# A two-layer memory-recurrent transformer block on Trainium2: the set-up's small transposes and first loads are moved, the weight loads are regrouped, and a new order table is used

## The chip, the core and the metric

The kernel runs on one NeuronCore of a Trainium2 chip. The metric is device time in microseconds (us) of one execution, from the runs' own timer; a profile of one further execution shows each engine's instructions. Engines: PE (matrix multiplications), DVE and ACT (vector and scalar work, here mostly copies out of PSUM, the layer norms and the softmaxes), POOL, and SP, which here only issues DMAs. DMAs move data between HBM and SBUF, or inside SBUF; some of them transpose on the way.

## The reference, cut to what matters

```python
def A(x, mem0):                      # 64 segments of 32 rows, one after the other
    mem = mem0                       # 8 rows
    for s in range(64):
        h = concat(mem, x[32*s:32*s+32])          # 40 x 448
        q, k, v = h @ Wq, h @ Wk, h @ Wv          # 16 heads of 256
        o = softmax(mask(q @ k.T / 16)) @ v @ Wo
        mem = o[:8];  out[32*s:32*s+32] = o[8:]
def B(x):                            # gated MLP, 448 -> 1792 -> 448
    return (relu(x @ W_gate) * (x @ W_up)) @ W_down
x = x + A(ln(x));  x = x + B(ln(x));  x = x + A(ln(x));  x = x + B(ln(x))    # x: 2048 x 448
```

The memory that segment s hands to segment s+1 makes A a recurrence: the second pass of A can only follow the first one, four segments behind.

## The kernel before

**Folded weights.** Each head's scores are h Wq Wk^T h^T, and each head's output is P h Wv Wo. So a *set-up* multiplies the weights once: 128 matmuls make M = Wq Wk^T (`prodM`), 128 make N = Wv Wo (`prodN`), each in four *quarters* of four heads. `products` (called in `setup`, L801 to L869) makes two products of a pair of heads at a time; a quarter is 24 matmuls on the whole PE array and 8 on half of its columns, and needs a quarter of both weights. The products are copied out of PSUM by ACT and DVE (L730, L731).

**Loads of the set-up.** Wq, Wk and Wv are loaded by transposing DMAs into eight slots of the tile `big` (`wT`, issued on L806), Wo by plain ones (`wo`, L810). A quarter is 0.9 MB. All are issued by SP, whose queue is in order: an instruction that waits holds back those behind it. Between the first loads SP also issues the first 64 rows of x (L788), the memory's two pieces (L789, L790), the transpose of the memory (L791), of the first normalised rows (L925, in `ln_a`) and of the first h (L1059, in `h_nat`). PE's work on a quarter of M waits for that quarter of Wq and of Wk.

**Steps.** After the set-up 68 steps follow; step t does segment t of the first layer and segment t-4 of the second. A step makes TT = M h (`t_units`: matmuls `P<-hT,Mw` and `P<-hT,M`), the scores of the memory rows (`P<-hT,TTm`) and of the segment rows (`P<-hT,TTs`), softmaxes on DVE and ACT, the memory's output (`P<-ident,Pm`, `P<-PTm,hK`, `P<-Nw,UTm`: "ptm", "umem" and "unm" below), its transpose back into hT (`P<-selm,X`, "mt"), and the segment's output (`P<-PTs,hK`, and for two steps at once `P<-Nw,big`). Each pair of steps also takes a tile of 128 rows through the MLP (`P<-xBT,big`, `P<-big,hB`). The next step's t_units need mt's result. In steps 12 to 59 the pattern repeats every four steps.

**What sets the order.** Each operation is recorded (`_Order.add`) with an estimated duration; a planner (`_Order.run`) then lays them out engine by engine. On PE the order goes by a table `RANK` written into the file, one number for each kind of operation and place; DVE, ACT, POOL and SP take, of the operations ready within `SLACK` ns, the one with the highest priority, which `BIAS` shifts by kind. An operation that may run on ACT or DVE goes to the one that the planner has free first. The engines then run their lists in order and wait for each other by semaphores. All PE instructions are written on L135.

**Tile forms.** PE's array is used whole (128*128 in the profile), as two halves of 64 rows (64*128), as two halves of columns (128*64) or as four strips of 32 columns (128*32); matmuls on different parts run at the same time. The planner's `mode` tells these apart.

**Transposes.** Rows and columns are exchanged either by a DMA that transposes, or on PE by a matmul with an identity matrix (`transposed`, L1048), whose result DVE copies out of PSUM. Before, PE does this only for tiles of the last steps.

Of the kernel before, what the change touches and what calls it, by code (L numbers as in the profile page):

```python
# [7 lines left out]
BF = dt.bfloat16  # L8
# [164 lines left out]
class _Order:  # L173
# [238 lines left out]
BIAS = {'dnE': 3176.0, 'glE': -82836.0, 'hk': 20613.0, 'init': 13859.0, 'lna': 7507.0, 'lnaC': -13533.0, 'lnaT': -43908.0, 'lnb': 29243.0, 'lnbT':  # L412
    -1363.0, 'load': 14359.0, 'mem': -10045.0, 'mt': -1168.0, 'mtE': 18941.0, 'prodE': -35100.0, 'ptmE': 12133.0, 'pts': -3736.0, 'ptsE': -5023.0,
    'ride': -1141.0, 'rt': -20763.0, 'rtT': -24105.0, 'smx': 110515.0, 'ssx': -8015.0, 'tEm': -15380.0, 'tEs': -51468.0, 'umE': -46772.0, 'usE':
    -102462.0, 'wg': -1137.0, 'x': -3626.0, 'xE': 55107.0, 'xb': -35016.0, 'yE': -13006.0, 'ys': 8416.0}
SLACK = {"pe": 108.0, "act": 154.0, "dve": 264.0, "pool": 233.0, "sp": 156.0}
PERIOD = 88192
RANK = {'dn.1': (-104610, 108209, -90484, -82188, -75463, -89082, -42692), 'dn.3': (-145101, -63706, -147288, -87906, -65974, -148521, -105677),
    'dn.e-1': (-141783, -142922, -108237, -138993, -143563, -144358, -145977), 'dn.e-3': (-104113, -71161, -102721, -97163, -97947, -76248, -66681),
    'dn.e1': (-82612, -70713, -79787, -45174, -88781, -40934, -62418), 'dnc.e1': (-96652, -57589, -80514, -147771, -97522, -72425, -17242), 'dnc.e3':  # L420
    (-146846, -103333, -121313, -81992, -86751, -107795, -123988), 'dnc.r1': (-117628, -111364, -73352, -38397, -118907, -118093, -32712), 'dnc.r3':
    (-143017, -137155, 18497, -94398, -143254, -115919, -116884), 'dnc.r5': (-106807, -76746, -107659, -97861, -105664, -60991, -110757), 'dnc.r7':
    (-144792, -138828, -146554, -77829, -119011, -118053, -123462), 'glF0.1': (-96461, -101197), 'glF0.3': (-127779, -127536), 'glF0.e-1': (-124566,
    -135911), 'glF0.e-3': (-95498, -95971), 'glF0.e1': (-31142, -52941, -93058, -94243), 'glF0.e3': (-100249, -61034), 'glF0.r1': (-112765, -113170),
    'glF0.r3': (-132135, -137757), 'glF0.r5': (-103453, -104429), 'glF0.r7': (-129942, -128688), 'glF1.1': (-21437, -96883), 'glF1.3': (-129957,
    -130626), 'glF1.e-1': (-128167, -130286), 'glF1.e-3': (-42210, -99667), 'glF1.e1': (-74197, -74754, -92380, -92606), 'glF1.e3': (-117239,
    -111385), 'glF1.r1': (-114358, -112556), 'glF1.r3': (-64652, -135836), 'glF1.r5': (-103077, -104009), 'glF1.r7': (-126468, -72866), 'glF2.1':
    (-99406, -102205), 'glF2.3': (-30063, -137144), 'glF2.e-1': (-135080, -136315), 'glF2.e-3': (-86341, -50884), 'glF2.e1': (-69414, -83802, -95776,
    -90525), 'glF2.e3': (-123487, -131166), 'glF2.r1': (-106583, -115805), 'glF2.r3': (-46676, -98801), 'glF2.r5': (-81661, -106213), 'glF2.r7':
    (-134619, -88043), 'glF3.1': (1334, -600), 'glF3.3': (-15610, -49583), 'glF3.e-1': (-67322, -113701), 'glF3.e-3': (-72200, -95812), 'glF3.e1':  # L430
    (-76155, -75823, -92586, -94517), 'glF3.e3': (-107149, -141187), 'glF3.r1': (-58559, -114450), 'glF3.r3': (-137836, -137979), 'glF3.r5': (-73882,
    -77471), 'glF3.r7': (-130187, -128436), 'glH0.1': (-95004,), 'glH0.3': (-126217,), 'glH0.e-1': (-125385,), 'glH0.e-3': (-95255,), 'glH0.e1':
    (-76562, -92759), 'glH0.e3': (-101751,), 'glH0.r1': (-111534,), 'glH0.r3': (-134652,), 'glH0.r5': (-102256,), 'glH0.r7': (-126926,), 'glH1.1':
    (-98081,), 'glH1.3': (-125139,), 'glH1.e-1': (-125229,), 'glH1.e-3': (-99371,), 'glH1.e1': (-73456, -90480), 'glH1.e3': (-21565,), 'glH1.r1':
    (-111459,), 'glH1.r3': (-137215,), 'glH1.r5': (-102039,), 'glH1.r7': (-131203,), 'glH2.1': (-95573,), 'glH2.3': (-136318,), 'glH2.e-1':
    (-133204,), 'glH2.e-3': (-102542,), 'glH2.e1': (-79422, -92762), 'glH2.e3': (-21556,), 'glH2.r1': (-115069,), 'glH2.r3': (-139483,), 'glH2.r5':
    (-102571,), 'glH2.r7': (-133536,), 'glH3.1': (-104497,), 'glH3.3': (-130453,), 'glH3.e-1': (-130004,), 'glH3.e-3': (-103143,), 'glH3.e1': (-73596,
    -43078), 'glH3.e3': (-95245,), 'glH3.r1': (-112910,), 'glH3.r3': (-136600,), 'glH3.r5': (-105539,), 'glH3.r7': (-127975,), 'lnbT.e3': (-97266,),
    'mt.0': (-48556,), 'mt.1': (-73646,), 'mt.2': (-87524,), 'mt.3': (-111081,), 'mt.e-1': (-110824,), 'mt.e-2': (-85897,), 'mt.e-3': (-72736,),
    'mt.e-4': (-46901,), 'mt.e0': (-47132,), 'mt.e1': (-64122,), 'mt.e2': (-82778,), 'mt.r0': (-116855,), 'mt.r1': (-91632,), 'mt.r2': (-103650,),  # L440
    'mt.r3': (-124373,), 'mt.r4': (-56759,), 'mt.r5': (-10709,), 'mt.r6': (-91148,), 'mt.r7': (-111361,), 'prodM.r0': (7632, 8758, 3519, 18670,
    -18035, -8559, -19521, 22221, 506, 0, 29137, -16498, 23379, -13694, -14382, -8950, -10525, -16874, -19468, -19177, 16859, -17615, -19884, -20323,
    -14282, -19681, -10489, -17286, -21816, -21722, -21526, -21195, -23854, -22964, -26122, -20647, -22523, -24653, -20618, -21769, -20688, -25891,
    -30330, -28270, -28128, -29016, -29523, -37170, -26079, -29040, -31310, -35312, -29785, -36941, -29896, -27348), 'prodN.r0': (-44880, -39246,
    -42485, -45500, -43952, -42650, -38039, -4352, -42711, 17370, -35502, -48417, -46709, -57726, -46225, -49325, -39689, -14687, -3938, -48290,
    -57916, -59747, -35946, 21060, -51553, -27452, -46795, -34885, -52124, -55744, -51211, -53783, -42693, -26175, -59523, -53826, -58085, -57316,
    -38263, -59020, -41416, -59756, -60059, -53961, -62863, -56473, -38442, -70119, -68178, -57790, -58316, -67893, -41999, -49426, -68908, -58622),
    'ptm.0': (-41321,), 'ptm.1': (-59656,), 'ptm.2': (-78783,), 'ptm.3': (-98083,), 'ptm.e-1': (-98891,), 'ptm.e-2': (-77845,), 'ptm.e-3': (-60297,),
    'ptm.e-4': (-41694,), 'ptm.e0': (-38279,), 'ptm.e1': (-55288,), 'ptm.e2': (-75058,), 'ptm.r0': (-51324,), 'ptm.r1': (-72642,), 'ptm.r2':
    (-98342,), 'ptm.r3': (-114034,), 'ptm.r4': (-49435,), 'ptm.r5': (-57665,), 'ptm.r6': (-86733,), 'ptm.r7': (-103757,), 'pts.e3': (-95739,),  # L450
# [912 lines left out]
```

## Time and profile before

| | |
|---|---|
| median of 6 runs | 1508.49 us (1504.79 to 1510.80) |
| the profiled execution: its own time | 1512.58 us |
| its span, first to last instruction | 1510.8 us |
| PE busy | 1459.3 us, 97% of the span |
| ACT, DVE busy | 802.8 us (53%), 778.0 us (51%) |
| idle time of PE that a wait for Wk's loads ended | 20.7 us, in 4 waits |
| first "unm" (`P<-Nw,UTm`) starts | 78.59 us |

The profile lists, by line and engine, how long instructions ran and what ended the idle time before them. Its timeline gives the start of each group of like instructions; "SPq" there is an issue by SP's queue, and its duration is that of issuing, not of the transfer. The chain of waits follows the run back from its last instruction. A view of windows gives each engine's busy time and PE's granted clock in a stretch (1.00 is full speed, 0.50 half). A busy PE isn't a PE at its peak, since the ends of matmuls are modelled; the distance between starts is what shows its pace.

### The profile page before, as it was taken

What the parts mean: (1) busy time and instruction counts of PE and PEld (TensorE: products, weight loads), DVE (VectorE), ACT (ScalarE), POOL (GpSimd) and SP (SyncE); (2) the same over time, 40 slices, a digit from 0 to 9 for tenths busy, and PEclk for the clock granted to TensorE, in tenths of its full rate; (3) what the DMA queues carried; (4) which work ended last, traced back from release to release, by engine and by line L of the source; (5) the groups of instructions that cost most, each with busy time, mean ns of one, the idle gap of its engine ahead of it and who ended that gap; (6) DMA issues with size and microseconds to landing.
All of it is one profiled execution on the core that took longest, in us unless ns stands there. A gap on an engine that the chain in (4) does not pass through costs nothing.

```text
span 1510.8 us, 79648 instructions
## 1 busy us (share of the span) xinstructions
PE 1459.3 (97%) x37086; PEld 1163.8 (77%) x37086; DVE 778.0 (51%) x2033; ACT 802.8 (53%) x2436; POOL 38.6 (3%) x86
## 2 busy tenths in 40 slices
PE   5889899999999999999999999999999999999997
PEld 2467778788878778788878778888878878887775
DVE  4434554555455455645455554545555555545553
ACT  4744556456554555556455545546455545645342
POOL 2000000000000000000000000000000000000000
PEclk9989999999999999999999999999999999999998
DMA  9942212112121121111121111111111111122121
GB/s 204 222 131 34 23 34 27 30 21 32 27 33 25 29 31 29 25 21 34 30 30 25 29 31 28 25 25 34 30 28 27 28 30 23 29 25 32 24 31 16
DMA packets 187547, 60.23 MB, mean 40 GB/s; under 512 B 176313, under 2 KB 186321, under 8 KB 187217
## 3 DMA queue, kind: packets, MB, share of 16 engines
q1 hardware_dynamic: 187216, 55.15, 20.8%
q8 instruction: 291, 4.77, 1.3%
q14 instruction: 40, 0.32, 0.1%
HBM read 10.33 MB, written 1.84 MB: 8 GB/s over the span
## 4 chain that ended last, share of the span: by engine, by line
PE 90%; DVE 3%; DMA 3%; SPq 2%; ACT 1%; issue 0%; POOL 0%
PE P L135 90%; SPq L806 2%; DMA PTs<-Ps 1%; DMA stg<-xnA 1%; DMA big<-in_A_Wk_dram 1%; DMA xBT<-xnB 1%; DVE XF L1215 1%; DVE stat L911 0%; ACT Mw L730 0%; DVE X L1129 0%; DVE hT L731 0%; DVE XA L1286 0%; DVE XB L1217 0%; DVE stat L984 0%; DVE big L731 0%
## 5 line engine op out<-in xcount | busy, mean ns | idle before, releaser
L135 PE MATMUL P<-hT,Mw 128*128 128x80 bf16 (+1 forms) x11424 | 423.4, 200 | 2.2 <-issue 2.0
L135 PEld LDWEIGHTS P<-hT,Mw 128*128 128x128 bf16 x11424 | 403.0, 100 | 12.1 <-issue 2.2
L730 ACT ACTIVATE TTs<-P 128x384 bf16<-128x384 f32 (+3 forms) x653 | 294.3, 451 | 0.0
L135 PE MATMUL P<-Nw,big 128*32 128x448 bf16 x5488 | 282.4, 353 | 0.5 <-issue 0.4
L730 ACT ACTIVATE TTm<-P 128x96 bf16<-128x96 f32 (+2 forms) x652 | 158.0, 242 | 171.0 <-PE P L135 160.4
L730 ACT ACTIVATE big<-P 128x512 bf16<-128x512 f32 (+1 forms) x367 | 185.0, 545 | 105.6 <-PE P L135 105.3
L135 PEld LDWEIGHTS P<-Nw,big 128*32 128x32 bf16 x5488 | 139.8, 97 | 98.7 <-issue 3.8
L135 PE MATMUL P<-xBT,big 128*128 128x128 bf16 (+3 forms) x3920 | 213.1, 216 | 1.5 <-DMA xBT<-xnB 0.9
L135 PEld LDWEIGHTS P<-xBT,big 128*128 128x128 bf16 (+1 forms) x3920 | 185.3, 98 | 19.5 <-issue 5.7
L135 PE MATMUL P<-Nw,UTm 128*32 128x224 bf16 x7504 | 194.3, 261 | 1.0 <-ACT UTm L730 0.6
L135 PEld LDWEIGHTS P<-Nw,UTm 128*32 128x32 bf16 x7504 | 179.9, 98 | 14.4 <-issue 4.3
L731 DVE CAST big<-P 128x512 bf16<-128x512 f32 (+1 forms) x145 | 87.7, 615 | 102.9 <-PE P L135 101.4
L1251 ACT ACTIVATE gT<-P 128x512 bf16<-128x512 f32 (+2 forms) x140 | 71.0, 509 | 91.7 <-DVE hB L1252 60.3
L984 DVE TENSOR_REDUCE stat<-P 128x2 f32<-128x80 f32 (+1 forms) x67 | 15.7, 234 | 196.6 <-PE P L135 195.2
L135 PE MATMUL P<-hT,M 64*128 64x80 bf16 (+1 forms) x3808 | 93.8, 197 | 8.7 <-DVE hT L731 4.3
L135 PEld LDWEIGHTS P<-hT,M 64*128 64x128 bf16 x3808 | 75.7, 96 | 27.1 <-issue 7.0
L135 PE MATMUL P<-big,hB 128*128 128x448 bf16 (+1 forms) x574 | 96.4, 354 | 0.0
L1129 DVE TENSOR_TENSOR X<-P,XH 32x224 bf16<-32x224 f32 x134 | 51.1, 381 | 87.3 <-ACT XH L1126 85.1
L135 PE MATMUL P<-PTs,hK 64*128 64x512 bf16 (+1 forms) x640 | 87.1, 338 | 3.5 <-DMA PTs<-Ps 3.3
L1126 ACT ACTIVATE XH<-P 64x224 f32<-64x224 f32 x67 | 23.6, 352 | 120.1 <-PE P L135 120.1
L1252 DVE TENSOR_TENSOR hB<-gT,P 128x512 bf16<-128x512 bf16 (+2 forms) x140 | 76.7, 575 | 17.8 <-ACT gT L1251 14.3
L135 PE MATMUL P<-big 128*128 128x448 bf16 (+1 forms) x256 | 50.7, 384 | 20.7 <-DMA big<-in_A_Wk_dram 20.7
(89 smaller groups left out, 1155.6 us busy)
## 6 DMA issues: line engine op xcount, KB each, us to landing
big<-in_A_Wo_dram SPq DMA_DIRECT2D x4, 896.0 KB, 7.1
XA<-in_A_x_dram SPq DMA_DIRECT2D x32, 56.0 KB, 2.3
out_dram<-ys SPq DMA_DIRECT2D x32, 56.0 KB, 2.3
big<-in_B_W_down_dram SPq DMA_DIRECT2D x2, 784.0 KB, 6.6
big<-in_B_W_gate_dram SPq DMA_DIRECT2D x3, 448.0 KB, 4.4
big<-in_B_W_up_dram SPq DMA_DIRECT2D x3, 448.0 KB, 4.2
hK<-hT SPq DMA_TRANSPOSE x68, 2.8
PTs<-Ps SPq DMA_TRANSPOSE x67, 3.0
```

Source lines behind the costliest of these rows:

```text
L135: ins = E.matmul(out, lhsT=lhsT, rhs=rhs, **kw)
L730: return E.activation(out(), src(), ACT.Copy)
L731: return E.tensor_copy(out(), src())
L806: wload(f"w{k}" + ("ab"[half] if half is not None else ""), lambda E: E.dma_start_transpose(dst, W[:, c:c + w]), [("slot", i, j) for i in ...
L984: S.dve(kind, lambda E: E.tensor_reduce(st[:, so:so + n], src(), AX.X, ALU.max), w, rd, [(pre, 0)])
L1126: S.act("xE", lambda E: E.activation(S.XH[64:128, :], T.b()[64:128, 0:224], ACT.Copy), 224, T.res(BOTQ), [("XH",)])
L1129: S.dve("xE", lambda E, r=r, r2=r2, c=c: E.tensor_tensor(S.X[r, c], T.b()[r, 0:224], S.XH[r2, :], ALU.add), 224, T.res((j,)) + [("XH",)], ...
L1215: S.dve("xb", lambda E: E.tensor_tensor(S.XF[r, :], T.b()[r, 0:D], S.XA[cols, q, :], ALU.add), D, T.res((TOPQ, BOTQ)[h]) + [("XA", q, l)], ...
L1251: S.act("glE", lambda E, G=G, k=k, w=w: E.activation(S.gT[:, k % 2, 0:w * n], G.b()[:, 0:w * n], ACT.Relu), w * n, G.res(), [("gT", k % 2)])
L1252: S.dve("glE", lambda E, V=V, k=k, w=w, a=a: E.tensor_tensor(S.hB[:, a:a + w, 0:n], S.gT[:, k % 2, 0:w * n].rearrange("p (i x) -> p i x", ...
```

## The change

- The first rows of x and the memory's two pieces are issued on ACT's queue instead of SP's, ahead of ACT's other work.
- The memory, the first normalised rows and the first h are transposed on PE (16, 128 and 128 columns at a time, five matmuls each) with a copy by DVE, instead of by DMAs that SP issues. `transposed` learns a form of 16 rows.
- Wq and Wk are loaded quarter by quarter in turn, instead of Wq's last two quarters in one; the last quarter of Wk comes in two halves with a semaphore each. Wv's first two quarters are two loads, with Wo's first two between them. The planner's estimates for loads are changed.
- `BIAS`, `SLACK` and `RANK` are replaced, and so is the order of all engines' instructions throughout the run. What is computed stays.

In the order as built, matmul by matmul: in steps 12 to 59 PE's 2188 matmuls of four steps are the same, in another order. SP's list in the set-up is Wq, Wk, Wq, Wk, Wq, Wk, Wq, Wk's two halves, a quarter of Wv, two of Wo, two of Wv, then PTs<-Ps of step 0 (L1052, waits for DVE), then the last two of Wo and Wv's halves. PE's list begins with the memory's five transposes, then the whole first quarter of M (24 and 8 matmuls), and goes on quarter by quarter; after M it does all of step 0's t_units and both its scores before N begins. Before, PE left the first quarter of M after 8 matmuls for one that needed the second.

```diff
+BIAS = {'dnE': 2862.0, 'first': 1181.0, 'glE': -38535.0, 'hk': 28128.0, 'hkE': 15263.0, 'init': 27046.0, 'lnaC': 24960.0, 'lnaT': 1106.0, 'lnaTE':
...
-SLACK = {"pe": 108.0, "act": 154.0, "dve": 264.0, "pool": 233.0, "sp": 156.0}
+SLACK = {"pe": 108.0, "act": 130.0, "dve": 225.0, "pool": 426.0, "sp": 337.0}
...
-        def small():
-            wload("x0", lambda E: E.dma_start(S.XA[0:64, 0, :], S.x_d[0:64, :]), [("XA", 0, 0)], 300.0, 2300.0)
...
-            S.dma("mem", "mT", lambda E: E.dma_start_transpose(S.mTc[:, :, :], mN), [("gT", 0), ("gT", 1)], [("mTc",)], 500.0, 6500.0, base=1e9)
+        def first(name, fn, wr):
+            S.dma("first", name, fn, (), wr, 500.0, 2600.0, "act", base=1e9)
+        first("x0", lambda E: E.dma_start(S.XA[0:64, 0, :], S.x_d[0:64, :]), [("XA", 0, 0)])
...
+        S.transposed("mT", mN, 640, S.mTc[:, :, :].rearrange("p k x -> p (k x)"), [("gT", 0), ("gT", 1)], [("mTc",)], rows=16)
...
-        wT(0, S.Wq_d, 0)
-        wT(2, S.Wk_d, 0)
-        small()
-        wT(1, S.Wq_d, 1)
-        wT(3, S.Wk_d, 1)
-        wT(4, S.Wq_d, 2, 2)
-        wT(6, S.Wk_d, 2)
-        wT(7, S.Wk_d, 3)
+        for q in range(4):
+            wT((0, 1, 4, 5)[q], S.Wq_d, q)
+            if q < 3:
+                wT((2, 3, 6)[q], S.Wk_d, q)
+        wT(7, S.Wk_d, 3, half=0)
+        wT(7, S.Wk_d, 3, half=1)
...
-        wT(0, S.Wv_d, 0, 2)
+        wT(0, S.Wv_d, 0)
         wo(2, 0)
         wo(3, 1)
+        wT(1, S.Wv_d, 1)
+        wT(4, S.Wv_d, 2)
         wo(6, 2)
-        wT(4, S.Wv_d, 2)
...
+        if p == 0:
+            S.transposed("lnaT", src, 640, dst.rearrange("p k x -> p (k x)"), keys, [("stg",)])
...
+        if t == 0:
+            S.transposed("hk", src, 640, S.hK[:, 0, :, :].rearrange("p k x -> p (k x)"), S.hkeys(b), [("hK", 0)])
```

## The prediction

> **What bounds the kernel now.** I read the page's busy shares first: PE 97%, so time can only come from PE's idle time, its clock, or its pace. The waits of PE name 20.7 us in four waits for Wk's loads, all in the set-up; then the timeline of SP and PE there, window rows for PE's clock, and the timeline of one stretch of the repeating steps. SP's queue in the set-up (start, duration of issuing):
>
> ```profile
> 4.35 4.04 SPq L806 DMA_TRANSPOSE big<-in_A_Wk_dram  x1
> 8.44 0.60 SPq L788 DMA_DIRECT2D XA<-in_A_x_dram  x1
> ...
> 9.97 3.59 SPq L806 DMA_TRANSPOSE big<-in_A_Wq_dram  x1
> 13.68 1.17 SPq L791 DMA_TRANSPOSE mTc<-gT  x1
> 14.89 3.51 SPq L806 DMA_TRANSPOSE big<-in_A_Wk_dram  x1
> 18.44 1.28 SPq L925 DMA_TRANSPOSE stg<-xnA  x1
> 19.76 7.03 SPq L806 DMA_TRANSPOSE big<-in_A_Wq_dram  x1
> 26.83 3.80 SPq L806 DMA_TRANSPOSE big<-in_A_Wk_dram  x1
> 30.68 1.28 SPq L1059 DMA_TRANSPOSE hK<-hT  x1
> 31.99 4.43 SPq L806 DMA_TRANSPOSE big<-in_A_Wk_dram  x1
> ```
>
> SP issues without a pause; a weight quarter takes it 3.5 to 4.0 us, and the small instructions between them 1.5, 1.2, 1.3 and 1.3 us. PE beside it, with what ended each idle time:
>
> ```profile
> 10.48 3.17 PE L135 MATMUL P<-big 128*128 128x448 bf16 x8 [10.48 <-DMA big<-in_A_Wk_dram]
> 20.48 11.85 PE L135 MATMUL P<-big 128*64 128x448 bf16 x56 [6.83 <-DMA big<-in_A_Wk_dram]
> 32.94 5.21 PE L135 MATMUL P<-big 128*128 128x448 bf16 x28 [0.62 <-DMA big<-in_A_Wk_dram]
> ```
>
> The fourth wait ends at 40.94 (2.79 us), as Wk's last quarter lands; 36 matmuls later M ends, at 48.5. From there to 78.59, where the first unm starts, PE has only one idle time (1.32 us, at 54.95, "issue"). So a microsecond taken from the loading of M is one taken from the run. In the repeating steps (12 to 59) an unm starts every four steps at a distance of 85.45 us (402.0, 487.4, 573.0), with hardly a wait:
>
> ```profile
> 402.00:487.40 85.40, 85.05 (x2189) 69.16 (x2188) 45.21 (x115) 46.47 (x140) 1.81 (x4) 1.00 0.19 28
> 408.03 0.59 PE L135 MATMUL P<-hT,M 64*128 64x80 bf16 x24
> 408.56 2.75 PE L135 MATMUL P<-hT,Mw 128*128 128x80 bf16 x72
> 411.24 0.75 PE L135 MATMUL P<-hT,M 64*128 64x80 bf16 x32
> ```
>
> The first line is a window row (length, then busy time of PE, PE's weight loads, DVE, ACT, POOL; clock; DMA), the others are PE's timeline. 72 matmuls of 80 columns start 36 ns apart, 2.59 us, yet the next group starts 2.68 us on: the change of tile form costs about 0.1 us. There, only fewer changes of form or fewer waits can save time.
>
> **Set-up: the loading of M.** The first two loads stay (landed 10.43). Then SP no longer issues the three first pieces (1.5 us), the memory's transpose (1.2), the rows' (1.3) and h's (1.3). With seven loads back to back at 3.55 to 3.85 us (rows 9.97 and 26.83) and Wk's halves at half of that, issuing of Wk's second quarter ends at 16.0, the third at 23.6, Wq's fourth at 27.4, the halves at 29.3 and 31.2. A load landed 2.0 to 2.3 us after its issue ended (8.39 to 10.43, 18.40 to 20.43, 30.63 to 32.89): 18.1, 25.8, 29.6, 31.4 and 33.4. One more thing stood in the way of the last load:
>
> ```profile
> GB/s 289 268 287 288 293 275 245 116 0 65 184 235 277 59 10 164 291 288 293 287 294 184 147 101 1 0 3 9 78 289 291 288 291 289 290 290 289 293 288 291
> ```
>
> That is 30 to 45 us in 40 slices: at 34.9 and from 38.7 to 40.3 the transfers stand still, each time just after a packet of instructions (8 to 16 KB) on another queue. Such a pause of 2 us may strike again, with Wk's halves in flight: I add 1 us to them.
>
> PE on M: 128 matmuls take 22.2 us at full clock (0.188 us apart, half-column ones in pairs), 5.5 a quarter. The first quarter starts at 10.43 at half clock. The starts were 0.374 us apart from 20.5 to 24.3, and 0.188 after:
>
> ```profile
> 20.40:24.30 3.90, 3.83 (x13) 1.38 (x14) 0.91 (x3) 1.78 (x5) 0.91 (x2) 0.51 0.85 190
> 24.30:32.40 8.10, 8.02 (x45) 3.20 (x43) 4.98 (x19) 7.77 (x24) 0.00 (x0) 1.00 1.16 260
> 40.90:44.80 3.90, 3.86 (x18) 1.53 (x19) 0.97 (x5) 2.51 (x7) 0.00 (x0) 0.56 1.28 290
> ```
>
> So 3.6 us at half clock cost 1.8 extra: quarter 1 ends at 10.43 + 5.5 + 1.8 = 17.7; quarter 2, from 18.1 with the rows' transposes (0.4), at 24.0; PE then waits 1.8 us for 25.8. Whether that gates the clock is open: a wait of 0.62 us (32.94) didn't, one of 2.79 us did (third row, 0.56). Between these ends, 0 and 1.8 us, I take 0.9. Quarter 3 with h's transposes: 25.8 + 5.9 + 0.9 = 32.6; the last quarter's first half to 35.4, its second, from 35.4 (landed 34.4), to 38.2. With some 0.7 us for waits on copies out of PSUM: **M ends at 38.9**, 9.6 us earlier; 37.5 without penalties, 41 with a 2 us pause and a full half-clock spell.
>
> A rule of the Trainium skill bears on the open point: TensorE: Matmul & The Clock Gate, "Part 1: The HAM clock gate", has PE fall to half clock after an idle window of about 3.4 us. By it the 1.8 us would be free and M would end 0.9 us earlier; the row at 40.90 shows half clock after only 2.79 us, so the rule is too mild for this trace, and I keep the bounds.
>
> **Set-up: from M to the first unm.** The work is the same (30.1 us from 48.5 to 78.59, the 1.32 us included). New: all of step 0's t_units stand ahead of N, with the scores right behind them. Nine of their ten results are copied by ACT, 0.45 us each (rows at 49.9 to 55.4), against 0.45 to 0.5 us on PE, so the scores wait about 0.7 us for the last. Nothing: the first pieces on ACT's queue (ACT has no other work before 10.4; a load of x landed 2 us after its issue, so the memory is there by some 6, PE's first instruction is free 4 us ahead of Wk; without that cover it would cost its delay) and the DVE copies of the transposes (three of under 0.5 us). What could be late next is N's weights: SP now holds the last two Wo quarters and Wv's last two halves behind PTs of step 0, which waits for its softmax (about 49). Before, from the end of Wk's last issue to the landing of the last load passed 30.8 us (36.4 to 67.2). From 31.2 that gives 62, with the wait for PTs 63 to 65; PE needs that last half at about 65 (38.9 + 30.1 + 0.7 - 2.9 for unm's wait and N's end). So nothing, up to 2 us. **First unm at 69.7: -8.9 us** (-12.3 to -4.5).
>
> **The order.** I counted changes of tile form in PE's list as built: 785 before, 756 after; in four repeating steps 44 and 41, -0.3 us. Of waits there is one of note before: in one step of four the t_units follow mt at once and wait 0.5 us; after, six PTs matmuls (0.45 us) stand between. On the other side two gaps shrink: between unm and mt from 2.15 us or more (one of 1.31) to 1.34 in another step, where X is written 1.49 us after the last unm's start; and between umem and unm from 1.65 to 0.97, where UTm's copies ended 0.8 to 1.3 us after umem. New waits of 0.2 to 0.5, so -0.1 in all, bounded by -0.55 (no wait left) and +0.6 (both gaps late, and a copy queued ahead). Per four steps **-0.4** (-0.85 to +0.3), in 12 such stretches **-4.8 us** (-10 to +3.6). In steps 0 to 11 the order has 3 changes fewer, in the last ones 5 more: +0.2. Their waits (18 us in steps 0 to 7 beyond streaming) are a chain of small steps that the order leaves as it was: unchanged, give or take 2.
>
> **Sum.** Against the profiled execution's 1512.6: -8.9 - 4.8 + 0.2 = -13.5. It lies 4.1 above the median of the runs; the difference is applied to the median: 1508.5 - 13.5 = **1495.0 us**.
>
> **Rivals.** (1) *The transfers, not SP's issues, set the pace of loading:* the gaps that the small DMAs left were time that the queues needed, and pauses return. For: the pauses above. Against: transfers ran at 290 GB/s within a load, and the slices between loads were empty. Then Wk lands at 37.5 instead of 33.4, M ends at 41.0 and N's last half is 2 us late: first unm at 73.8, -4.8 for the set-up, with -4.6 for the order 1499.1. (2) *The order gains nothing:* the three changes are paid back in waits on DVE, which gets 122 instead of 115 operations in four steps. For: the shorter gaps. Against: DVE is busy 53% there. 1508.5 - 8.9 = 1499.6. (3) *Slower:* in the repeating steps UTm's and X's copies come behind other copies in ACT's and DVE's lists (a 512-column copy is 0.5 to 0.6 us), both short gaps miss, and mt, hence the next step, is late. It outweighs the set-up from 1.3 us of new waits in four steps (12 x 1.3 = 15.6 against 8.9 + 3.7 + 3.0 for the bound); at 1.5 us, 1514. Against: two gaps of twelve of the recurrence shrink, each by under 1 us.
>
> **Chances.** Forecast 0.62, (1) 0.14, (2) 0.17, (3) 0.07. The range runs from the set-up's and order's good ends together (1508.5 - 12.3 - 10 = 1486) to the set-up's bad end with nothing from the order (1503.9): 1486.5 to 1503. Measurements of this kernel tell about 0.2% (3 us) from no change. Faster by over 0.2%: the forecast, nearly all of (1), most of (2), 0.89; within 0.2%: 0.05; slower: 0.06.
>
> **What would show it.** Right: first unm near 69.7; PE's idle time for Wk down from 20.7 to 12 to 14 us, of which 10.4 is the start; M's end at 38 to 40; stretches of four steps at 85.0 instead of 85.45. Wrong: Wk's last landing past 37 (1); stretches at 85.4 (2) or 86.7 and more, with PE waiting for X or UTm (3); N waiting for Wv or Wo, which would mean that PTs on SP's queue costs what I took as free.

## The result, and the profile after

The kernel after takes **1501.81 us** (median of 18 runs, 1497.96 to 1506.64) against 1509.34 us for the kernel before (median of the 40 runs beside it): a ratio of 0.9953, 95% interval 0.9944 to 0.9962, or -7.1 us (-8.5 to -5.7). That is faster, as forecast, but by about half of the forecast 13.5 us, and above the 1499 that both milder rivals gave, though inside the range (1486.5 to 1503). The profiled execution took 1503.20 us, its span is 1501.4.

SP's queue in the set-up after (timeline; start, duration of issuing):

```profile
16.64 3.63 SPq L809 DMA_TRANSPOSE big<-in_A_Wq_dram  x1
20.31 4.08 SPq L809 DMA_TRANSPOSE big<-in_A_Wk_dram  x1
24.43 4.44 SPq L809 DMA_TRANSPOSE big<-in_A_Wq_dram  x1
28.91 4.32 SPq L809 DMA_TRANSPOSE big<-in_A_Wk_dram  x2
33.27 3.97 SPq L809 DMA_TRANSPOSE big<-in_A_Wv_dram  x1
37.29 1.21 SPq L813 DMA_DIRECT2D big<-in_A_Wo_dram  x2
38.54 13.36 SPq L809 DMA_TRANSPOSE big<-in_A_Wv_dram  x2
55.52 1.19 SPq L1052 DMA_TRANSPOSE PTs<-Ps  x1
56.75 1.21 SPq L813 DMA_DIRECT2D big<-in_A_Wo_dram  x2
```

The small instructions between the loads are gone, and Wk's last issue ends at 33.2 instead of 36.4. PE beside it:

```profile
10.63 6.92 PE L135 MATMUL P<-big 128*128 128x448 bf16 x32 [4.77 <-DMA big<-in_A_Wk_dram]
18.76 3.58 PE L135 MATMUL P<-big 128*128 128x448 bf16 x18 [1.20 <-DMA big<-in_A_Wk_dram]
...
26.43 2.44 PE L135 MATMUL P<-big 128*128 128x448 bf16 x12 [1.80 <-DMA big<-in_A_Wk_dram]
...
33.91 5.82 PE L135 MATMUL P<-big 128*128 128x448 bf16 x32 [1.61 <-DMA big<-in_A_Wk_dram]
40.84 0.62 PE L135 MATMUL P<-hT,M 64*128 64x40 bf16 x36 [1.11 <-ACT M L732]
41.39 2.87 PE L135 MATMUL P<-hT,Mw 128*128 128x40 bf16 x108
44.20 0.42 PE L135 MATMUL P<-hT,M 64*128 64x40 bf16 x20
44.55 1.17 PE L135 MATMUL P<-hT,Mw 128*128 128x40 bf16 x40
47.91 0.83 PE L135 MATMUL P<-hT,Mw 128*128 128x40 bf16 x20 [2.19 <-issue]
49.02 0.35 PE L135 MATMUL P<-hT,TTm 128*128 128x40 bf16 x5 [0.29 <-ACT TTm L732]
...
75.33 2.87 PE L135 MATMUL P<-Nw,UTm 128*32 128x224 bf16 x112
```

M's last matmul starts at 39.4 (48.2 in the profile before): nearly as forecast. But the first unm starts at 75.33 and not at 69.7. Between the two stand things that were not forecast: a wait of 1.11 us for ACT's copies of M's last quarter, one of 2.19 us marked "issue" (the profile shows nothing that PE waited for) in the middle of step 0's t_units, and then PE's clock. Window rows of the kernel after (length, then busy time of PE, PE's weight loads, DVE, ACT, POOL; clock; DMA), the first three in the set-up, the last one four of the repeating steps:

```profile
47.90:49.70 1.80, 1.50 (x39) 1.38 (x39) 0.65 (x4) 0.37 (x2) 0.00 (x0) 0.50 0.93 210
49.70:54.30 4.60, 4.60 (x18) 1.66 (x14) 2.33 (x9) 2.64 (x6) 0.00 (x0) 0.50 0.94 192
54.30:58.80 4.50, 4.50 (x27) 1.98 (x27) 2.28 (x5) 3.43 (x8) 0.00 (x0) 1.00 0.24 43
...
398.70:483.60 84.90, 84.80 (x2196) 68.86 (x2188) 47.17 (x123) 45.32 (x133) 1.82 (x4) 1.00 0.17 29
```

From 47.9 to 54.3 the clock is at half; PE is busy for 6.1 us of it, so this costs about 3.1 us. Four repeating steps take 84.90 us (85.40 in the row shown before); PE's idle time in them fell from 0.35 to 0.10 and its busy time by 0.25.

**By stages.** Distances between starts of unm, from all profiles of the two kernels and of the two half changes (next section); a stage is named by its steps:

| us | before | before, 2nd profile | set-up only | order only | after | after, 2nd | after, 3rd |
|---|---|---|---|---|---|---|---|
| M's last matmul | 48.20 | 43.34 | 39.52 | 45.26 | 39.38 | 41.68 | 39.81 |
| first unm | 78.59 | 75.20 | 75.77 | 76.82 | 75.33 | 77.97 | 75.01 |
| steps 0-3 | 74.09 | 71.69 | 71.57 | 72.44 | 72.23 | 70.47 | 71.16 |
| steps 4-11 | 163.74 | 163.90 | 163.91 | 163.42 | 166.22 | 164.42 | 164.73 |
| steps 12-57 | 979.97 | 979.95 | 979.67 | 972.83 | 972.28 | 973.67 | 974.20 |
| steps 58-61 | 85.98 | 86.07 | 85.99 | 89.22 | 90.39 | 89.59 | 90.16 |
| 62 to the last matmul | 124.26 | 121.47 | 122.50 | 122.02 | 120.77 | 121.79 | 121.14 |

Three things are to be read from it. The repeating steps gain 5.5 to 7.7 us, more than forecast, in every profile of the new order. Steps 58 to 61 lose 3 to 4.4 of them again. And the first unm, where 8.9 us were forecast, is hardly earlier.

### The profile page after: what moved, and what is told of

It is laid out like the page before. It is cut to its first block, busy times and chain, and to the rows that moved or that the text cites. A ratio compares the mean times of both kernels' runs of the same rounds, so it can differ in the third digit from the quotient of the medians.

```text
span 1501.4 us, 79751 instructions
## 1 busy us (share of the span) xinstructions
PE 1456.7 (97%) x37101; PEld 1159.4 (77%) x37101; DVE 802.3 (53%) x2123; ACT 789.2 (53%) x2349; POOL 38.6 (3%) x86
## 4 chain that ended last, share of the span: by engine, by line
PE 91%; DVE 2%; ACT 2%; DMA 2%; SPq 2%; issue 1%
PE P L135 91%; SPq L809 2%; DMA xBT<-xnB 1%; ACT big L732 1%; DMA PTs<-Ps 1%; DVE X L1139 0%; DMA big<-in_A_Wk_dram 0%; ACT Mw L732 0%; ACT TTm L732 0%; DVE xnB L920 0%; ACT TTs L732 0%; DVE stat L913 0%; ACT XH L1136 0%; ACT UTm L732 0%; DVE stat L994 0%
## 5 line engine op out<-in xcount | busy, mean ns | idle before, releaser
L732 ACT ACTIVATE TTs<-P 128x384 bf16<-128x384 f32 (+2 forms) x595 | 269.8, 454 | 0.0
L732 ACT ACTIVATE TTm<-P 128x96 bf16<-128x96 f32 (+3 forms) x623 | 150.9, 242 | 172.6 <-PE P L135 158.8
L732 ACT ACTIVATE big<-P 128x512 bf16<-128x512 f32 (+1 forms) x358 | 173.5, 533 | 81.4 <-PE P L135 77.9
L733 DVE CAST big<-P 128x512 bf16<-128x512 f32 (+1 forms) x154 | 99.6, 649 | 55.3 <-PE P L135 53.6
L135 PE MATMUL P<-big,hB 128*128 128x448 bf16 (+1 forms) x574 | 97.9, 353 | 0.0
L733 DVE CAST TTm<-P 128x64 bf16<-128x64 f32 (+2 forms) x57 | 12.9, 226 | 117.7 <-PE P L135 117.6
```

The source lines that it names most:

```text
L135: ins = E.matmul(out, lhsT=lhsT, rhs=rhs, **kw)
L732: return E.activation(out(), src(), ACT.Copy)
L733: return E.tensor_copy(out(), src())
```

## The experiments

Times in one table; each ratio is to the kernel before, run beside it.

| run | median us | before us | ratio, 95% interval |
|---|---|---|---|
| set-up only | 1505.48 | 1505.84 | 0.9995 (0.9983 to 1.0006) |
| order only | 1501.80 | 1505.84 | 0.9970 (0.9959 to 0.9980) |
| after, again | 1499.90 | 1505.84 | 0.9959 (0.9944 to 0.9974) |
| PTs after the loads | 1498.56 | 1506.06 | 0.9950 (0.9932 to 0.9968) |
| N among the t_units | 1497.88 | 1506.06 | 0.9949 (0.9931 to 0.9967) |
| both of these | 1498.15 | 1506.06 | 0.9947 (0.9928 to 0.9966) |
| loads alternate, PTs after | 1499.60 | 1506.46 | 0.9954 (0.9938 to 0.9970) |
| loads alternate | 1501.58 | 1506.46 | 0.9959 (0.9943 to 0.9974) |
| last rows of before | 1511.05 | 1506.46 | 1.0031 (1.0018 to 1.0044) |
| before, again | 1506.04 | 1506.46 | 0.9997 (0.9985 to 1.0009) |
| two t_units early, loads alternate, PTs after | 1495.66 | 1505.22 | 0.9934 (0.9920 to 0.9948) |
| the same, again | 1500.76 | 1508.89 | 0.9941 (0.9925 to 0.9956) |
| two t_units early | 1501.16 | 1508.89 | 0.9946 (0.9930 to 0.9961) |
| after, a third time | 1501.97 | 1508.89 | 0.9958 (0.9942 to 0.9975) |
| pattern four steps longer | 1517.15 | 1505.22 | 1.0084 (1.0067 to 1.0102) |

### The two halves of the change, and the kernel after again

```diff
# set-up only: the kernel after, but
-BIAS, SLACK, RANK of after
+those of before; rows of the set-up and step 0 (.r0) of RANK and BIAS of the new kinds from after
# order only: the kernel before, but
-BIAS, SLACK, RANK of before
+those of after; rows of the set-up and step 0 of RANK from before
```

> The changed kernel's set-up (its loads, its transposes on TensorE and its order up to the first unm), with the order tables of before for all later steps. Theory (the set-up gave less than forecast, the order more in the repeating steps and a loss near the end): first unm at 75 to 76, about 3 us earlier than before, stretches of four steps at 85.45 as before, time 2 to 4 us under before (ratio 0.9975 to 0.9985). Rival (the set-up gave its 9 us, and the order lost what is missing): time 8 to 10 us under before (0.9935 to 0.9945).

> Set-up of before with the changed kernel's order tables from the first unm on. Theory: first unm at 78 to 79 as before; stretches of four steps at 84.9; some 7 us gained in steps 12 to 57 and some 4.5 lost in steps 58 to 61, in all 3 to 6 us under before (0.996 to 0.998). Rival (order lost): 1 to 3 us over before.

> The changed kernel once more, as it is, beside the two others on the same chip. Theory: 0.9945 to 0.996 of before; in the profile first unm near 75, and TensorE short of instructions for 1 to 2.5 us in step 0's t_units once more, since the place is set by the count of instructions, not by chance. Rival (that stall and the half clock after it were chance): no such stall, first unm at 71 to 72.

The set-up alone is worth -0.8 us (-2.6 to +0.9): nothing that can be told from zero, and less than the 2 to 4 us expected of it. The order alone gives -4.5 (-6.2 to -3.0). Both together, run beside them, give -6.2 (-8.4 to -3.9). So most of the gain is the order's. With the set-up's edits M does end earlier (its last matmul starts at 39.5 against 45.3 with the old set-up), and the first unm is still only 1 us earlier. The second profile of the kernel after has M's end at 41.7, a wait "issue" of 3.08 us, and its first unm at 77.97. The question became where the 6 us go between M and the first unm.

### Before, again

The same kernel, for a second profile.

> The kernel before once more, for a second profile. Theory (the first profile's 2 us pause of the transfers just as Wk's last quarter landed, and so its end of M at 48.2 and its first unm at 78.6, was a chance of that execution): M ends at 45 to 46.5, the first unm starts at 76 to 77.5, as in the kernel with the old set-up and the new order; the set-up's edits are then worth 1 to 2 us to the first unm and not the 3.3 that the two first profiles show. Rival (the pause belongs to the old list of loads): pause again, M ends at 48 or later, first unm at 78 or later. The time itself: 1505 to 1509 by the runs.

The theory held, and more than held. PE's timeline in this second profile of the kernel before:

```profile
37.73 5.97 PE L135 MATMUL P<-big 128*64 128x448 bf16 x36 [0.24 <-DMA big<-in_A_Wk_dram]
43.63 0.75 PE L135 MATMUL P<-hT,M 64*128 64x40 bf16 x36
44.56 2.87 PE L135 MATMUL P<-hT,Mw 128*128 128x40 bf16 x108 [0.18 <-ACT Mw L730]
47.36 0.42 PE L135 MATMUL P<-hT,M 64*128 64x40 bf16 x20
47.71 0.62 PE L135 MATMUL P<-hT,Mw 128*128 128x40 bf16 x18
49.77 1.31 PE L135 MATMUL P<-big 128*128 128x448 bf16 x6 [1.44 <-DMA big<-in_A_Wo_dram]
50.92 1.21 PE L135 MATMUL P<-hT,Mw 128*128 128x40 bf16 x42
51.97 3.79 PE L135 MATMUL P<-big 128*128 128x448 bf16 x20
...
59.97 9.22 PE L135 MATMUL P<-big 128*128 128x448 bf16 x56 [1.00 <-DMA big<-in_A_Wv_dram]
...
75.20 2.87 PE L135 MATMUL P<-Nw,UTm 128*32 128x224 bf16 x112
```

Wk's last quarter landed at 37.7, not at 40.9. The transfers pause here too (2 to 10 GB/s from 39.8 to 40.9), but only after this landing: that the pause struck it was a chance of the first execution. There is no wait for instructions and no half clock up to the first unm, which starts at 75.20, the same as after. M's end (43.3) and the first unm are even earlier than was expected. In this list N's products stand between the t_units and after the scores; the kernel after has the t_units in one piece.

### PTs behind the loads, and N's products among the t_units

```diff
# PTs after the loads (L1053), the kernel after otherwise
-              1200.0, 3400.0, base=None if t else 1e9)
+              1200.0, 3400.0, base=None if t else 9e7)
# N among the t_units: RANK, units 3 and 4 of step 0 and both scores behind the first N products
-'tH3.r0': (-44000,), 'tF3.r0': (-44600, -44610), 'tH4.r0': (-44300,), 'tF4.r0': (-44900, -44910),
-'smem.r0': (-45410,), 'sseg.r0': (-45450,),
+'tH3.r0': (-45600,), 'tF3.r0': (-45700, -46100), 'tH4.r0': (-46400,), 'tF4.r0': (-46500, -46900),
+'smem.r0': (-47900,), 'sseg.r0': (-48300,),
```

> The changed kernel with one move: on SP's queue PTs of step 0 comes after the last loads of Wo and Wv instead of ahead of them, where SP waited 3.6 us for the softmax. Theory (TensorE never waits for those loads in the changed kernel): the last load lands 3 to 4 us earlier, at about 66, the first unm stays within 1 us of 75.3, the time within 1.5 us of the changed kernel's. Rival (N is paced by these loads): first unm and time 2 to 3.6 us earlier.

> The changed kernel with one move on TensorE: six products of N are put among the last t_units of step 0 and ahead of its scores, so that no long run of 25 ns matmuls stands there. Theory (the stall for instructions, the half clock behind it and the wait for the copies cost some 4.5 us, of which the last load, landing at 69.7, lets 2.6 be gained): no idle time for instructions over 0.5 us before the first unm, first unm at 72.5 to 73.5, time 1.5 to 3 us under the changed kernel. Rival (they are hidden behind the loads): first unm and time as in the changed kernel.

> Both moves together. Theory: the loads no longer bound it, so first unm at 70.5 to 72, time 3 to 5 us under the changed kernel. Rival: no better than the better of the two alone.

With PTs behind the loads the last load landed at 63.5 instead of 69.6, and the first unm started at 74.21; the wait marked "issue" was 2.30 us, and the time is not told apart from that of the kernel after. So N's loads are not what holds the first unm back. With N's products among the units the wait was 2.95 us and the first unm at 74.50: the theory that the long run of short matmuls brings the wait about fell. With both edits: 2.29 us, first unm 73.68.

### The loads in another order

PE's instructions come in blocks. The page counts the packets of the queue that fetches them (packets, MB, share):

```profile
q8 instruction: 291, 4.77, 1.3%
```

That is 16 KB in each. PE has 2 x 37101 matmuls and weight loads and some 440 waits in its list, and 291 x 256 is within one packet of that, so a packet holds 256 instructions. Counted in PE's list, its waits included, the wait stands ahead of the same instruction, number 706, in every profile that has it before the first unm; the later waits of this name in the kernel after stand at whole multiples of 256 behind it, so that 706 is a boundary of blocks. In the kernel after the fetch came 3.1 us after PE had entered the block ahead, just as the second of two plain Wo loads had landed. The theory was that those two loads held it up.

```diff
-        wo(3, 1)
         wT(1, S.Wv_d, 1)
+        wo(3, 1)
```

> The kernel after with two edits: SP's list of loads is Wv, Wo, Wv, Wo, Wv, Wo, Wo, Wv's halves, so that no two plain Wo loads stand next to each other while PE works on step 0's t_units; and PTs of step 0 follows all loads. Computes the same. Theory (PE runs out of instructions in step 0's t_units since their fetch comes only when the plain loads ahead of it have landed, 3 to 5 us after PE asked; the half clock of the N products behind it is its consequence): with only one plain load ahead of it the fetch comes 1.5 us earlier or more, the stall there shrinks from 2.2 to 2.3 us to under 0.8, the N products run at full clock at once, first unm at 70.5 to 72 (kernel after 75.3, with PTs moved alone 74.2), time 2 to 3 us under the kernel after. Rival A (any load in flight delays the fetch): stall of 2 us or more again, first unm 74 to 74.5. Rival B (the stall goes, but the chain of the first step, not PE, sets the first unm): stall gone, first unm 73.5 or later.

> The kernel after with the order of loads alone changed (Wv, Wo, Wv, Wo, Wv, then PTs of step 0, Wo, Wo, Wv's halves). Computes the same. Theory (fetch behind two plain loads): as for the run with both edits as far as the stall goes (under 0.8 us instead of 2.2), first unm at 71.5 to 73; last load lands at 68 to 70 as in the kernel after. Rival: stall of 2 us or more, first unm 75 to 75.5.

The theory fell: 2.50 and 2.52 us, the fetch 3.3 us late with one plain load ahead of it, too. Rival A stands: in this stretch it is late under any of these loads.

### Two t_units in the wait for Wk

If the order of loads can't bring the fetch earlier, the block ahead can be made longer, or the work done elsewhere. Step 0's t_units are cut by quarters of M, and the two that need only the first two quarters go into PE's wait for the third quarter's Wk.

```diff
# t_units, for t == 0 and k < 4 (unit k of four, 6 of M's 28 column groups each)
-            for j in range(a, z)
+            js = [8 * c + 2 * k + e for c in range(3) for e in range(2)]      # rows of M's quarter k
-            S.hkeys(b) + S.Mkeys
+            S.hkeys(b) + [("M", h, kt) for h in range(4 * k, 4 * k + 4) for kt in range(3)]
# RANK
-'tH0.r0': (-42200,), 'tF0.r0': (-43100, -43110),  (and unit 1)
+'tH0.r0': (-24000,), 'tF0.r0': (-24010, -24020),  (and unit 1)
```

> The kernel with the loads alternating and PTs behind them, and one more edit: step 0's t_units are cut by quarters of M instead of by rows, so that two of five need only M's first two quarters; these two (2 x 1.25 us of short matmuls) are put into PE's wait for Wq's third quarter, before M's third quarter. Computes the same. Theory (what the set-up's edits won at M's end was lost in step 0's t_units: the wait for copies of M's last quarter, PE out of instructions, half clock behind that; a PE that has half of this work done earlier and goes from M into long N products loses little of it): M ends at 39 to 40.5, PE's idle time between M's end and the first N product under 2 us (4.2 in the kernel with alternating loads), first unm at 70 to 72 instead of 74.8, time 2.5 to 4.5 us under that kernel's. Rival A (N's loads set the pace as soon as PE is early): waits for Wv and Wo of 1 us or more twice, first unm 72.5 or later. Rival B (the first unm is not what the end of the run hangs on: steps 0 to 11 give it back): first unm at 70 to 72 but time within 1 us of the kernel with alternating loads.

PE's timeline of this kernel (loads alternating, PTs behind them, two units early):

```profile
24.78 0.32 PE L135 MATMUL P<-hT,M 64*128 64x40 bf16 x12
25.03 1.07 PE L135 MATMUL P<-hT,Mw 128*128 128x40 bf16 x36
26.03 0.32 PE L135 MATMUL P<-hT,M 64*128 64x40 bf16 x12
26.28 1.07 PE L135 MATMUL P<-hT,Mw 128*128 128x40 bf16 x36
28.43 2.44 PE L135 MATMUL P<-big 128*128 128x448 bf16 x12 [1.08 <-DMA big<-in_A_Wk_dram]
...
40.88 0.32 PE L135 MATMUL P<-hT,M 64*128 64x40 bf16 x12
41.13 1.07 PE L135 MATMUL P<-hT,Mw 128*128 128x40 bf16 x36
42.13 0.42 PE L135 MATMUL P<-hT,M 64*128 64x40 bf16 x20
42.48 1.67 PE L135 MATMUL P<-hT,Mw 128*128 128x40 bf16 x60
...
44.99 5.81 PE L135 MATMUL P<-big 128*128 128x448 bf16 x32
52.13 1.31 PE L135 MATMUL P<-big 128*128 128x448 bf16 x6 [1.33 <-DMA big<-in_A_Wo_dram]
...
70.25 2.87 PE L135 MATMUL P<-Nw,UTm 128*32 128x224 bf16 x112
```

The wait marked "issue" is gone, the wait for copies of M too, the clock stays full from 16.3 to 77.8 us, and the first unm starts at 70.25, near what the forecast had promised for the change itself. But this kernel isn't the forecast one: some 2.5 us of t_units now run in PE's wait for Wk. What is left are short waits for N's weights (1.33 and 0.42). Three more runs ask which edit did it, and what it is worth.

> The kernel after with one edit: step 0's t_units cut by quarters of M, two of the five put into PE's wait for Wk's third quarter; the list of loads and PTs of step 0 as in the kernel after. Computes the same. Theory (the set-up's gain was lost at the place of these t_units: out of instructions, half clock, wait for copies): the stall and the half clock before 60 us go with this edit alone, as they went with all three edits together; first unm at 70.5 to 72.5, the last load landing at 66 to 69 makes it a little later than the 70.25 there; time 1.5 to 3.5 us under the kernel after in the same call. Rival (the loads' order was needed too: with the last loads behind PTs, N waits for them): first unm at 73 or later with a wait for Wv or Wo of 2 us or more in PE's last N quarter.

> The kernel with the three set-up edits (loads alternating, PTs behind them, two t_units early) once more, for a second profile and for a comparison with the kernel after on one chip. Theory: first unm at 70 to 71 again, no wait for instructions and no half clock before 65 us; time 4 to 6 us under the kernel after. Rival (the 2 to 3 us that steps 0 to 7 took longer in its first profile, with 6.8 us of half clock from 84.6 on, belong to it): steps 0 to 3 take 72 us or more again, time 2 to 3 us under the kernel after.

> The kernel after once more, beside the other two. Theory: PE out of instructions for 2 to 3.5 us at 46 to 51 us, then half clock, M's end at 39 to 42, first unm at 75 to 78; steps 58 to 61 take 89.5 to 90.5 us; ratio to the kernel before 0.994 to 0.997. Rival (the stall was a chance of the two profiles of this kernel): no stall above 1 us before the first unm.

On the kernel after, the early units alone do the same to the wait and to the clock; the first unm starts at 71.67, held by N's weights (3.9 us of waits), as the rival said in part:

```profile
51.22 1.31 PE L135 MATMUL P<-big 128*128 128x448 bf16 x6 [1.11 <-DMA big<-in_A_Wv_dram]
...
59.84 2.44 PE L135 MATMUL P<-big 128*128 128x448 bf16 x12 [2.75 <-DMA big<-in_A_Wo_dram]
...
71.67 2.87 PE L135 MATMUL P<-Nw,UTm 128*32 128x224 bf16 x112
```

In the second profile of the kernel with all three edits the first unm starts at 71.33, with three waits for Wo (0.98, 1.31 and 0.73 us), and again without the wait for instructions. The third profile of the kernel after has that wait again (2.30 us) and its first unm at 75.01. Side by side, by the trace: when PE entered the block that ends at instruction 706, when the packet of the next block came, when the block's work was done, and when PE went on.

| us | enters | packet | done | goes on | wait |
|---|---|---|---|---|---|
| after | 42.4 | 45.5 | 45.7 | 47.9 | 2.19 |
| after, 3rd | 42.8 | 46.0 | 46.1 | 48.4 | 2.30 |
| loads alternate, PTs after | 42.4 | 45.7 | 45.7 | 48.2 | 2.50 |
| N among the t_units | 42.2 | 47.0 | 46.7 | 49.6 | 2.95 |
| before | 50.7 | 53.8 | 54.9 | 56.3 | 1.32 |
| order only | 47.8 | 51.4 | 53.4 | 53.6 | 0.26 |
| before, 2nd | 46.0 | 48.9 | 51.7 | 51.7 | none |
| units early, loads alternate | 37.5 | 39.9 | 43.5 | 43.5 | none |
| units early alone | 36.7 | 39.8 | 42.7 | 42.7 | none |

Wherever PE waited at this place it went on 2.2 to 2.7 us after the packet; the packet came 2.4 to 4.8 us after the block was entered (0.3 in one more profile, the second of the kernel with all three edits, where PE didn't wait either); and a block that lasted 5.7 us or more never ran dry. In steps 12 to 59, 256 instructions last 5.0 us on average (4376 in 85 us) and the packet comes 0.4 us after the entry (median). The block of t_units in one piece lasts 3.3 us; with N's products among them it lasted 4.5, and the fetch came 4.8 us late. That is what the change did: it put the short matmuls into one block, at a time when the fetch is late.

The half clock goes with this wait. All eleven profiles that have it for 2.2 us or more have a spell of half clock of 3.4 or 6.8 us there, beginning between 47.0 and 50.4; the other six have none between 45 and 77. And these two, with the waits for copies and loads, make nearly the whole difference between the kernels in this stretch: from the start of M's last matmul to the first unm less PE's waits and half of its busy time at half clock, 28.9 to 29.8 us are left in all fourteen profiles with the t_units behind M, old set-up or new, and 27.6 to 27.8 with two of the units early.

In the time, the early units alone give -0.8 and all three edits -1.2 us against the kernel after run beside them, where 1.5 to 3.5 and 4 to 6 were expected; neither is told apart from nothing. Over all runs the three-edit kernel stands at 0.9934 and 0.9941 of the kernel before, the kernel after at 0.9953, 0.9959 and 0.9958. The best estimate from these, some 2 to 3 us, is less than the 3.3 to 4.8 us at the first unm (against the third profile of after), and its size stays open: the second profile had no half clock before 77 us and still lost 1.0 us twice to waits for instructions, at 97.9 and 112.2.

### The last steps

```diff
# last rows of before: RANK of the kernel after, but
-rows .e-4 to .e3 (steps 60 to 67) of after
+those of before
# pattern four steps longer: RANK of the kernel after, but
-rows .e-4 to .e-1 (steps 60 to 63)
+rows .0 to .3, those of the repeating pattern
```

> The kernel after with the rank rows of the last eight steps (60 to 67) taken from the kernel before, the other rows, BIAS and SLACK from after. Computes the same. Theory (the 3.6 to 4.4 us that the new order loses at the end of the repeating pattern, steps 58 to 61, belong to the new rank rows of the last steps): steps 58 to 61 take 86 to 87 us instead of 90.4, steps 62 on stay within 1 us of before's 87.4, time 2 to 3 us under the kernel after. Rival (the loss is of the seam: old and new rows don't fit each other, or the loss is of the DVE and ACT order): steps 58 to 61 stay at 89 us or more, or the following steps take it back; time as the kernel after or above.

> The kernel after with one edit in the table: the rank rows of steps 60 to 63 are those of the repeating pattern, so that the pattern goes on for four more steps, up to the last one that has a segment of both layers. Computes the same. Theory (the new rows of steps 60 to 63 are what loses 3.6 to 4.4 us at the end of the pattern): steps 58 to 61 at 85 to 86 us instead of 90.4, the seam to the last four steps then costs no more than 1 us, time 2.5 to 4 us under the kernel after. Rival (the loss is of any seam from the pattern to the last steps: the work of the MLP that is left over must be done somewhere): what steps 58 to 61 gain, steps 62 to the end lose; time within 1 us of the kernel after, or above.

Both theories of a cure fell. With before's rows steps 58 to 61 take 98.2 us. With the pattern for four steps more they take 85.0, as expected, but then the MLP stands behind: PE waits for the transposed rows of one of its tiles, and for 24 us runs at half clock (the timeline, then a window row).

```profile
1408.74 1.04 PE L135 MATMUL P<-xBT,big 64*128 64x128 bf16 x16 [5.91 <-DMA xBT<-xnB]
...
1405.00:1430.00 25.00, 17.61 (x333) 14.45 (x334) 2.70 (x8) 5.45 (x22) 0.00 (x0) 0.52 0.03 7
```

Steps 62 to 65 take 112.2 us there. So both kernels pay more for the seam between the pattern and the last steps, and of the three with the new pattern the one with its own last rows pays least, 3 to 4.4 us. That the pattern leaves work over for the last steps would explain it; no run shows that by itself. Where they pay is seen in the kernel after, first its row for steps 58 to 61, then the two waits in it for copies by DVE that hold up the memory's chain:

```profile
1286.10:1376.50 90.40, 87.65 (x2204) 69.51 (x2200) 47.42 (x121) 47.17 (x138) 1.82 (x4) 1.00 0.16 26
...
1335.62 2.87 PE L135 MATMUL P<-Nw,UTm 128*32 128x224 bf16 x112 [0.73 <-DVE UTm L733]
...
1362.22 0.29 PE L135 MATMUL P<-selm,X 128*128 128x32 bf16 x5 [0.53 <-DVE X L1139]
```

and the same steps in the second profile of the kernel before:

```profile
1290.70:1376.80 86.10, 85.60 (x2196) 69.27 (x2188) 45.63 (x117) 46.28 (x139) 1.82 (x4) 1.00 0.20 27
```

PE's idle time is 2.75 us against 0.50, and it is busy 2.05 us longer: there are 52 changes of tile form instead of 47, some 0.5 us at 0.1 each, and 8 matmuls `P<-Nw,big` more fall into the stretch, some 0.4 us; the other 1.1 us or so are not accounted for. Of the 2.25 us more idle time 1.26 are the two short gaps of rival (3), UTm and X, not in the repeating steps but in the one place where the order doesn't repeat; they come with the same lengths in all four profiles of the new order in the table. Another 0.67 is a wait marked "issue" that only two of the four have.

## Why the prediction was wrong

**The sign and the order: right, with a size too small.** The term was -0.4 us in four steps, -4.8 in all. Measured: -0.55 (85.45 to 84.90), and -6.6 over steps 12 to 57 (979.9 as the mean of the three profiles of the old order in the table, 973.3 of the four of the new). The forms agree with their size (-0.3; PE's busy time fell by 0.25). The waits don't: the 0.1 taken for them was 0.25, since the new waits that were set against the half microsecond behind mt are nearly absent.

**The last steps: wrong.** "+0.2", five changes of form at 0.1 each less the three fewer in steps 0 to 11. Steps 58 to 61 cost 3.8 us on average; the steps from 62 on are 1.3 faster, which is less than the 2.8 by which the old order's own profiles differ there. Forms were counted there; waits and the two short gaps were looked at in the repeating steps alone.

**The loading of M: nearly right.** Forecast: Wk's last half lands at 33.4 plus 1 for pauses, M ends at 38.9. Measured: 35.6, and M's last matmul starts at 39.4 to 41.7 in the three profiles of the kernel after. The issue of Wk's last half ended at 33.2 instead of 31.2, a loss of 2 us, about half of what rival (1) had as its whole: a quarter took 3.6 to 4.4 us of issuing where 3.55 to 3.85 were taken, though the view in the prediction has rows of 4.04 and 4.43 as well. Up to M's end PE waited 15.0 us, 9.4 for Wk and 5.6 for the memory's rows, where 12 to 14 were forecast.

**From M to the first unm: the step that failed.** "The work is the same (30.1 us from 48.5 to 78.59, the 1.32 us included)". The work is the same, but in the kernel after it took 36.0 us from the start of M's last matmul (39.38 to 75.33), in the profile before 30.4. So the prediction's sentence that a microsecond taken from the loading of M is one taken from the run didn't hold. Of the 5.6 us between the forecast first unm (69.7) and the measured one, 0.8 is M's end (0.3 us behind the start of its last matmul); 0.6 is waiting for copies (1.11 + 0.29, where 0.14 of the old stretch and the 0.7 allowed on top were in the sum); 0.9 is PE out of instructions (2.19 instead of the 1.32 in the old stretch); 3.1 is the half clock behind that; the small rest is left over. That was within sight: the 1.32 us marked "issue" in the profile before was carried along as a constant, without asking what makes it, though the change moves exactly the instructions around it. The early units bear the cause out: with two of the units elsewhere the wait, the half clock and the wait for copies go together, and the first unm starts at 70.25 to 71.67, though part of this is the work moved into the wait for Wk.

**The base: the second half of that failure.** The forecast took its -8.9 us from one execution and applied it to the median, having noted that this execution lay 4.1 us above it. Part of the excess lay in the very stretch that the change shortens: the second profile of the kernel before, 8.3 us shorter in all, has its first unm 3.4 us earlier (it is also 2.4 us shorter in steps 0 to 3 and 2.8 from step 62 on). Against the old set-up's three first unms (78.59, 75.20, 76.82; mean 76.9) the forecast 69.7 is -7.2, and what the new set-up got in its six (75.77, 75.33, 77.97, 75.01, 75.58, 75.88; mean 75.9) is -1.0.

**The rivals.** (1) was half there: the pauses returned. Wq's last quarter landed at 32.4 (forecast 29.6), 3.5 us after its issue ended. The transfers in the kernel after from 24 to 39 us, in 40 slices:

```profile
GB/s 283 289 291 290 238 53 164 311 201 9 12 272 291 289 290 290 344 86 32 214 27 109 291 290 271 251 290 290 275 165 181 248 291 287 202 244 289 291 267 77
```

They stand nearly still from 27.4 to 28.1 and falter from 30.4 to 32.2, both times just behind packets of instructions (at 26.96 and 30.37). But N wasn't held up by its loads. (2) was wrong: the order gains in the repeating steps, and it is the set-up that doesn't. (3) didn't come. What neither had was a gain at M's end that is spent on the way to the first unm. The free items were free in the kernel after: the first pieces on ACT's queue, DVE's copies of the transposes, and PTs ahead of N's last loads (moving it brought the loads 6 us forward and the time nothing that can be measured). The last was free while PE came late. The forecast had N's last load landing at 63 to 65 and needed at about 65 (its own terms add up to 66.8); it landed at 69.6. With the early units alone, and this list of loads, it is N's weights that hold the first unm at 71.67: PE waits 1.11 and 2.75 us for them. So the forecast's 69.7 was probably out of reach with this list even without the wait for instructions; no run shows that by itself.

**By terms**, in us:

| term | forecast | measured |
|---|---|---|
| set-up, to the first unm | -8.9 | -1.0 by the profiles, -0.8 (-2.6 to +0.9) by the run with the set-up alone |
| steps 12 to 57 | -4.8 | -6.6 |
| steps 0 to 11 and 58 to the end | +0.2 | +2.5: nothing in 0 to 11, +3.8 in 58 to 61, -1.3 from 62 on |
| sum | -13.5 | -7.1 (-8.5 to -5.7) |

The measured terms are means of three to six single executions that differ by 1 to 3 us. They add up to -5.1; the 2 us to -7.1 are within what such profiles can tell, and stay unexplained. The two halves run alone add up to -5.3, beside -6.2 for the kernel after in the same comparison.

## What to carry to other kernels

A wait marked "issue" is a cost with a cause, not a constant: here it was the fetch of instructions. When a change moves short instructions together, count the instructions in a fetch block and ask how long the block lasts against the fetch. Where a profile lies above the median of the runs, look for the stretch that holds the excess before a gain is taken from it; a second profile of the same kernel settles it for the price of one run. And what is won at one point of a chain is a gain only at the next point where the engine waits for nothing else.

## What the runs showed of the hardware that was not expected

**Instruction fetch can hold PE up.** PE's instructions came in packets of 16 KB, 256 instructions each, and PE waited 2.2 to 3.7 us at one boundary in each of the eleven profiles with the new set-up and step 0's t_units behind M. The Trainium skill, "Runtime: NRT & Kernel Launch", section "Instruction fetch mechanics", describes blocks of this size, fetched by the sequencer's own DMA queue while the last one executes, and a cost that is mostly hidden. The size agrees with the 291 packets here; nearly hidden it was in the repeating steps, and not among the set-up's loads. Why it is late there is not settled: the order of the loads makes no difference, and the load in flight at the time was a plain one in some kernels and a transposing one in others.

**The clock fell after waits shorter than expected.** PE's granted clock was 0.50 from 47.9 on, after waits of 1.11 and 2.19 us with work between. With waits of 1.44 and 1.00 us, some 10 us apart (the second profile of before), it stayed at 1.00, and so it did through waits of 1.11 and 2.75 us with the early units alone:

```profile
50.00:60.00 10.00, 6.15 (x36) 2.63 (x35) 2.38 (x5) 5.82 (x12) 0.00 (x0) 1.00 0.97 254
```

So the length of a single wait doesn't decide it. The Trainium skill, "TensorE: Matmul & The Clock Gate", "Part 1: The HAM clock gate", has the clock fall after an idle window of about 3.4 us that runs freely; the spells here last 3.4 us or twice that, which fits a window of such a length, but no wait ahead of this spell was that long.

**The same kernel differs between executions by more than the edits are worth in a stretch.** First unm at 78.59 and 75.20 for the kernel before, at 75.33, 77.97 and 75.01 for the kernel after, with 3.4 us spells of half clock at other places each time.
